# Attention's products of four pairs in one visit, 55 tanh differences by accumulating DMAs, exponentials summed on ScalarE

## The chip, the cores and the metric

One NeuronCore of a Trainium2 chip runs the whole kernel. The metric is device time in microseconds (us), from the start of the execution to its end. TensorE multiplies matrices; VectorE (DVE), ScalarE (ACT) and GpSimd (POOL) work elementwise; SyncE (SP) issues most DMAs, and POOL issues the DMAs that add to their destination. Each engine works off its own list of instructions in the order in which the program wrote them.

## The reference

Attention over chunks of 64 tokens, then a feed-forward network whose activation is h - tanh(h):

```python
scores = scale * np.matmul(q_c, k_c.transpose(0, 1, 2, 4, 3))   # per head and chunk, 64 x 64
scores = scores - np.max(scores, axis=-1, keepdims=True)
attn = np.exp(scores)
attn = attn / (np.sum(attn, axis=-1, keepdims=True) + 1e-09)
x = np.matmul(attn, v_c)          # to 4608 tokens x 512 (8 heads of 64)
h = x @ w_in                      # 512 -> 2048
g = h - np.tanh(h)
out = g @ w_out                   # 2048 -> 512
```

## The kernel before

**Tiles.** The 4608 tokens are 36 pairs of chunks (128 tokens each), and four pairs form a group; there are nine groups. A number is kept as a sum of two 16-bit floats, so a product takes three matmuls. Groups 2 to 8 compute x @ w_in by Winograd's scheme: a unit (four per group, so units 8 to 35) has seven products (`gx` to `gw`, 12 matmuls of 128x256 each, line 798) that gather in three PSUM banks X, Y and Z. Four chunks n = 4 unit + 0..3 of 128x512 numbers are then made from the banks.

**A chunk's steps.** `sc` (ScalarE copies one bank), `st` (VectorE adds bank X), `sn` (ScalarE's tanh), `su` (the difference h - tanh, line 837 on VectorE), `sh` and `sl` (high and low half for the next product, ScalarE and VectorE). For a chunk in the list `ADDED` the difference is no VectorE instruction: a DMA issued by POOL adds the (negated) tanh to the chunk in SBUF (line 836), the copy and the sum apply the scale instead, and tanh runs without one. The second product is `K` (groups 2 to 4, 6 matmuls of 128x512, line 955) or, in groups 5 to 8, again seven Winograd products: sums of chunks `na`, their halves `nh` and `nl`, products `kp` (6 matmuls of 128x256, line 901) and joins `kj` (lines 914 and 917).

**Attention of a late pair p (8 to 35).** `S` computes the scores: 32 matmuls of 64x64 into both banks of the PSUM tile psa (line 208). `m` takes the row maxima on VectorE, `E` the exponentials on ScalarE, `z` divides by the row sums on VectorE, `h` and `l` split into halves, `t` transposes by DMA, `V` multiplies by the values: 48 matmuls of 64x64 (line 449), from pair 12 on into banks X and Y. Four drains `X p.0` and so on move the result from X and Y to SBUF on ScalarE (line 461). Bank Z is the first bank of psa, so a unit's first product into Z (`gz`) waits until the scores in psa have been read, and `gy` and `gx` wait for the drains.

**Two ways to the exponentials.** For a pair in `SUMMED`, ScalarE reads the scores from PSUM head by head: eight exponentials with the maximum as bias, each summing its row (line 402), which leaves VectorE the maxima (line 391) and a small scaling (line 393). For the others VectorE first subtracts the maxima from PSUM into SBUF (line 395), ScalarE takes one exponential of 128x512 in SBUF (line 404), and VectorE sums the rows (line 410).

**The order** is written out by hand as the string `SECOND`: each engine receives its instructions in the order of the tokens, whatever the other engines do. A visit is called here a stretch of 64x64 matmuls on TensorE between matmuls of 128x128. From pair 12 on before has 29 visits: three of them hold the values of two pairs and the scores of the next two (`V12 V13 S14 S15`, and the same for 14 to 17 and 16 to 19); of the other 26 one holds two pairs' values and one pair's scores, four hold two pairs' values, two hold two pairs' scores, eight hold the values of one pair and eleven the scores of one pair.

**Blocks of w_out.** `te` (blocks_out) stores differences of weight blocks to DRAM, `tr` and `tx` (blocks_back) read them back, two DMAs each.

Of the kernel before, what the change touches and what calls it, by code (L numbers as in the profile page):

```python
# [14 lines left out]
F16 = mybir.dt.float16  # L15
# [6 lines left out]
P = 128  # L22
# [8 lines left out]
FC = DFF // P  # L31
# [10 lines left out]
UNITS = 4  # L42
# [16 lines left out]
ORDER = (0, 1, 3, 6, 9, 5, 7, 10, 8, 2, 4, 13, 15, 14, 12, 11)  # L59
BESIDE = 12  # L60
MORE, SUMS, BLOCKS, TURNED, CS = 0, 4, 8, 12, 14
SUMMED = (8, 9, 10, 11, 24, 25, 26, 27, 28, 29, 30, 31, 32, 33, 34, 35)
SEVEN = (5, 6, 7, 8)
ADDED = [n for n in range(64, 132) if n % 4 in (0, 1)]
RELOADED = range(24, 36)
# [24 lines left out]
def attn_ffn_kernel(ctx: ExitStack, tc: tile.TileContext, qkE, vE, qL, kL, vL, w_in, w_out, out):  # L90
# [8 lines left out]
    nc = tc.nc  # L99
# [11 lines left out]
    wt, half_w, w_pool = [[None, None] for _ in range(FC)], [[None] * FC for _ in range(2)], {}  # L111
# [13 lines left out]
    def freed(k, dtype=F16):  # L125

        return place_of("h", 1, ORDER[k], dtype)
# [3 lines left out]
    def new_x():  # L131
        return tuple(xpool.tile([P, KC, MOST], F32R, name=f"x{a}") for a in "hl")
# [170 lines left out]
    class Late:  # L303
# [81 lines left out]
        def less(self, p):  # L385
# [5 lines left out]
            nc.vector.reduce_max(out=mx.rearrange("p (hp u) one -> p hp (u one)", hp=4), in_=d["ps"], axis=AX.X)  # L391
            if p in SUMMED:
                nc.vector.tensor_scalar_mul(mx, mx, -scale)
# [3 lines left out]
        def exponents(self, p):  # L397
            d = self.st[p]
            s = d["s"]
            if p in SUMMED:  # L400
                for h in range(H):
# [4 lines left out]
        def shares(self, p):  # L406
            d = self.st[p]
            s, sm = d["s"], d["sm"]
            if p not in SUMMED:
                nc.vector.reduce_sum(out=sm[:, :, 0], in_=s, axis=AX.X)  # L410
# [72 lines left out]
    class Half:  # L483
# [93 lines left out]
        def blocks_out(self, j):  # L577
            t = self.t16[j].rearrange("p a (k n) -> p a k n", k=4)
            nc.sync.dma_start(out=half_w[0][2 * j + 1][:, :, :2 * P], in_=t[:, :, 0])
            nc.sync.dma_start(out=turned_out[:, j], in_=t[:, :, 1:])  # L580

        def blocks_back(self, u, k):

            for s in range(2):
                nc.sync.dma_start(out=self.block(u, s, k), in_=turned_out[:, 2 * (u % UNITS) + s, :, k - 1])
# [177 lines left out]
    class Winograd:  # L763
# [21 lines left out]
        def middle(self, unit):  # L785
            self.m5 = late.tile([P, MOST], F32, name="m5", bufs=1)
            if 4 * unit + 3 in ADDED:
                nc.scalar.activation(self.m5, self.banks["Z"], AF.Copy, scale=self.ff(4 * unit).sig)
# [24 lines left out]
        def copied(self, n):  # L813
            if n % 4 < 3:
                c, bank = self.place(n)[0], self.banks["YZY"[n % 4]]
                if n in ADDED:
                    nc.scalar.activation(c, bank, AF.Copy, scale=self.ff(n).sig)
# [3 lines left out]
        def summed(self, n):  # L821
            c = self.place(n)[0]
            other, op = self.m5 if n % 4 == 3 else c, ALU.subtract if n % 4 == 2 else ALU.add
            if n in ADDED:
                nc.vector.scalar_tensor_tensor(out=c, in0=self.banks["X"], scalar=self.ff(n).sig, in1=other, op0=ALU.mult, op1=op)
# [3 lines left out]
        def tanh(self, n):  # L829
            t = self.now[n][2] = ffn.tile([P, MOST], F32, name="t", bufs=3)  # L830
            nc.scalar.activation(t, self.now[n][0], AF.Tanh, scale=-1.0 if n in ADDED else self.ff(n).sig)

        def less(self, n):
            c, _, t, _ = self.now[n]
            if n in ADDED:
                return nc.gpsimd.dma_start(out=c, in_=t, accum_op=ALU.add)  # L836
# [166 lines left out]
    spots = Spots()  # L1003
    x, nx = new_x(), new_x()
# [63 lines left out]
    def add(h, l):  # L1068

        if len(adding) >= PACE:  # L1070
            nc.gpsimd.tensor_copy(tick, adding[-PACE])
        nc.gpsimd.dma_start(out=h, in_=l, accum_op=ALU.add)  # L1072
        adding.append(h[:1, :1] if len(h.shape) == 2 else h[:1, 0, :1])

    def whole_x():
        add(nx[0].bitcast(F32), nx[1].bitcast(F32))

    def late_parts():
        raw_pool.close()
        pool = ctx.enter_context(tc.tile_pool(name="att", bufs=1, side="right", reuse_waits="tile"))  # L1080
        early_psum.close()
        side = ctx.enter_context(tc.tile_pool(name="side", bufs=1, reuse_waits="tile"))
        dram = ctx.enter_context(tc.tile_pool(name="dram", bufs=1, space=bass.MemoryType.DRAM))
        return side, dram, pool, ctx.enter_context(tc.tile_pool(name="ps_a", bufs=1, space=PSUM, side="right", reuse_waits="tile"))

    with tc.manual_schedule(engines={E.SP, E.PE, E.DVE, E.Activation, E.Pool}):
        nc.scalar.activation(pool.tile([P, 1], F32, name="tiny", bufs=1), warm[:, :1], AF.Exp)
        wholes = {}
        for token in PLAN.split():
            if token[0] == "W":  # L1090
                if token == "Wx":
                    whole_x()
                else:
                    part, fc = map(int, token[1:].split("."))
                    h, l = (t.bitcast(F32) for t in wt[fc][part])
                    add(h, l)
                    wholes[part, fc] = h
            else:
                step(token)
        side, dram, late, ps_a = late_parts()  # L1100
        turned_out = dram.tile([P, FC // 2, 2, 3, 2 * P], F16, name="turned")
        parked = dram.tile([P, UNITS, 7, 2, 2, 2 * P], F16, name="parked")
        ps_o2 = pools[0]
        att, half = Late(late), Half(late)
        for (part, fc), h in wholes.items():
            half.w[part][fc] = h
        sums_w16 = [{} for _ in range(UNITS)]
        spare = late.tile([P, DM], F32, name="spare", bufs=1)
        before, x, sources = ff, nx, nx
        own.update({(0, 2): lambda: spare, (1, 0): lambda: freed(15, F32)})  # L1110
        x = tuple(nx[1].bitcast(F16).rearrange("p kc n -> p (kc n)").rearrange("p (a kc n) -> a p kc n", a=2, kc=KC)[a] for a in range(2))
        nx = new_sums_of_x()
        now = dict(x=nx)

        def second(g_):
            ff = now["ff"] = FeedForward(1, x)
            ff.room(ps_o1, range(2))
            ff.room(ps_o2, range(2, 4))
# [49 lines left out]
        def stage(name):  # L1168
            return lambda *n: getattr(now["w"], name)(*n)

        steps = dict(
            wA=half.tops, wB=half.powers, x=top, Q=third, ff=ready, xA=lambda: att.tops(1), xB=lambda: att.powers_of_tops(1), f=lambda: second(1), M=more,
            Cx=x_high, Dx=x_low, e=lambda t: before.scaled(t), o=lambda t: before.store(t),
            W=half.whole, C=lambda part, fc: half.convert(part, fc, (0,)), D=lambda part, fc: half.convert(part, fc, (1,)),
            G=lambda fc: now["ff"].gemm1(fc, 0, 4), P=lambda fc: now["ff"].gemm2((fc, 0)),
            i=lambda fc: now["ff"].tanh((fc, 0)), j=lambda fc: now["ff"].less((fc, 0)), k=lambda fc: now["ff"].high((fc, 0)), q=lambda fc: now["ff"].low((fc, 0)),
            a=att.load, v=att.load_values, u=att.largest, rA=att.tops, rB=att.powers_of_tops, s=att.split_high, d=att.split_low,
            S=att.scores, m=att.less, E=att.exponents, z=att.shares, h=att.shares_high, l=att.shares_low, t=att.turned, V=att.products,
            ee=lambda g, t: (now["ff"] if g == 1 else now["w"].ffs[g]).scaled(t), oo=lambda g, t: (now["ff"] if g == 1 else now["w"].ffs[g]).store(t), fb=power_of_third,
            gz=product("Z", 3, 3, True), gy=product("Y", 1, 1, True), gx=product("X", 0, 0, True), gu=product("Z", 6, 2), gv=product("X", 4, 4), gw=product("Y", 2, 6, True), gq=product("X", 5, 5),  # L1180
            mc=stage("middle"), K=stage("chunk"), sc=stage("copied"), st=stage("summed"), sn=stage("tanh"), su=stage("less"), sh=stage("high"), sl=stage("low"),
            ta=half.blocks_in, tb=half.blocks_sum, tc=half.blocks_split, te=half.blocks_out, tr=half.blocks_back, tx=lambda unit: half.blocks_back(unit, 1), wp=half.park, wl=stage("reload"), wn=half.norm_of_values, wr=half.norms_of_values, wt=half.largest_row, ww=half.norm_of_weights, wg=half.norm_of_g,
            na=stage("sum"), nh=stage("sum_high"), nl=stage("sum_low"), kp=stage("seventh"), kj=stage("join"), ks=stage("store"),
            X=result, T=half.sum, c=lambda u, k: half.slot(u, k, (0,)), b=lambda u, k: half.slot(u, k, (1,)))
        for token in SECOND.split():
            if token[0] == "0":
                step(token[1:])
                continue
            kind, numbers = re.fullmatch(r"([a-zA-Z]+)([\d.]*)", token).groups()
            steps[kind](*(int(n) for n in numbers.split(".") if n))  # L1190


# [43 lines left out]
```

## Time and profile before

| | before |
|---|---|
| time, median of 3 runs | 777.9 us (777.27 to 778.21) |
| the profiled execution's own time | 777.72 us |
| its span, first to last instruction | 775.7 us |
| TensorE matmuls busy | 763.6 us, 98% |
| VectorE busy | 693.5 us, 89% |
| ScalarE busy | 549.3 us, 71% |
| GpSimd busy | 77.4 us, 10% |

The profiled execution took 2.0 us more than its span, the part outside the first and last instruction. Matmuls overlap one another: a 128x256 one is shown 273 ns long and a 128x512 one 379 ns, and the next starts before it ends, so TensorE's busy share says little, and times on TensorE are better taken from start to start. Instructions of VectorE and ScalarE overlap a little too.

### The profile page before, as it was taken

Reading aid. Unit: us, or ns where it says so; the run is one execution under the profiler, and the core shown is the slowest. Engines: PE = TensorE matmul, PEld = TensorE weight load, DVE = VectorE, ACT = ScalarE, POOL = GpSimd, SP = SyncE. Lnnn points to the kernel's source line nnn. Section 1 sums busy time; section 2 is a strip of 40 time slices with the busy share of each in tenths; the row PEclk is TensorE's granted clock in tenths of the full one; section 3 lists DMA queues with packets and bytes.
Section 4 is the critical chain, followed back from the end, with each engine's and each line's share of the span. In section 5 each row is a group of like instructions: output and inputs, shape, how many; then the busy total and the mean of one; then the engine's idle time right before and its main releaser. Section 6 shows DMA issues by size and latency. Waiting matters only on the chain.

```text
span 775.7 us, 19620 instructions
## 1 busy us (share of the span) xinstructions
PE 763.6 (98%) x7895; PEld 568.6 (73%) x7898; DVE 693.5 (89%) x1302; ACT 549.3 (71%) x1229; POOL 77.4 (10%) x117
## 2 busy tenths in 40 slices
PE   8999999999999999999999999999999999999998
PEld 3777885444476666667676767878888888888887
DVE  7999999999999998999999989999978896889761
ACT  6989887877566665666566869786968586777631
POOL 0022235300000000000110020101010001010000
PEclk9999999999999999999999999999999999999999
DMA  9977978733142403414857887578499459565111
GB/s 352 363 211 202 255 185 168 146 91 97 41 97 52 127 2 93 139 56 124 242 160 210 247 194 173 137 179 213 131 252 176 130 136 246 137 165 171 60 42 55
DMA packets 102123, 121.35 MB, mean 156 GB/s; under 512 B 36368, under 2 KB 59280, under 8 KB 101904
## 3 DMA queue, kind: packets, MB, share of 16 engines
q1 hardware_dynamic: 92240, 101.67, 43.9%
q0 software_dynamic: 9648, 18.35, 14.2%
q8 instruction: 62, 1.02, 0.5%
q14 instruction: 29, 0.24, 0.1%
q10 hardware_dynamic: 144, 0.07, 0.0%
HBM read 73.40 MB, written 19.92 MB: 120 GB/s over the span
## 4 chain that ended last, share of the span: by engine, by line
PE 84%; issue 8%; DMA 3%; DVE 3%; POOL 1%; ACT 1%; SPq 1%; POOLq 0%
PE ph L798 20%; PE po L955 16%; PE po L901 14%; PE po L726 11%; PE ph L681 11%; PE psa L798 8%; PE psa L208 2%; DMA gl<-t 1%; DMA v<-vE 1%; PE ph L449 1%; PE ps L208 1%; PE ph L1052 1%; DMA rawv<-vL 0%; POOL wh L836 0%; PE ps L199 0%
## 5 line engine op out<-in xcount | busy, mean ns | idle before, releaser
L798 PEld LDWEIGHTS <-wh 128*128 128x128 f16 x1344 | 130.9, 98 | 22.6 <-issue 2.0
L798 PEld LDWEIGHTS <-wl 128*128 128x128 f16 x1008 | 98.0, 98 | 17.8 <-issue 1.0
L798 PE MATMUL ph<-xh,wl 128*128 128x256 f16 x576 | 97.7, 273 | 0.0
L798 PE MATMUL ph<-xh,wh 128*128 128x256 f16 x544 | 92.7, 273 | 1.0 <-DVE gl L827 0.5
L798 PE MATMUL ph<-xl,wl 128*128 128x256 f16 x288 | 78.5, 273 | 0.0
L798 PE MATMUL ph<-xl,wh 128*128 128x256 f16 x272 | 74.2, 273 | 0.0
L901 PE MATMUL po<-wl,wh 128*128 128x256 f16 x564 | 72.1, 273 | 1.1 <-ACT wh L860 0.5
L901 PEld LDWEIGHTS <-wh 128*128 128x128 f16 x660 | 63.7, 98 | 9.6 <-ACT wh L860 0.8
L955 PE MATMUL po<-wl,gl 128*128 128x512 f16 x288 | 68.3, 379 | 0.0
L955 PE MATMUL po<-wl,gh 128*128 128x512 f16 x288 | 68.3, 379 | 0.0
L726 PE MATMUL po<-wl,gh 128*128 128x512 f16 (+1 forms) x192 | 63.3, 384 | 0.0
L798 PE MATMUL psa<-xh,wh 128*128 128x256 f16 x352 | 60.0, 273 | 0.2 <-ACT s L402 0.2
L955 PEld LDWEIGHTS <-gl 128*128 128x128 f16 x288 | 27.6, 98 | 29.0 <-DVE gl L851 0.2
L798 PE MATMUL psa<-xl,wh 128*128 128x256 f16 x176 | 48.0, 273 | 0.0
L955 PEld LDWEIGHTS <-gh 128*128 128x128 f16 x288 | 27.7, 98 | 27.4
L681 PE MATMUL ph<-xl,wl 128*128 128x512 f16 x192 | 43.1, 380 | 0.0
L402 ACT ACTIVATE s<-psa,mx 128x64 f32<-128x64 f32 x128 | 38.1, 338 | 2.2 <-DVE from L148 1.5
L466 DVE TENSOR_TENSOR xl<-wh,xh 128x512 f16<-128x512 f32 (+1 forms) x56 | 34.2, 617 | 2.0 <-ACT xh L466 1.8
L466 ACT CAST xh<-wh 128x512 f16<-128x512 f32 (+1 forms) x56 | 31.3, 575 | 5.5 <-DVE wh L474 3.9
L914 ACT ACTIVATE wh<-po,undo_g 128x256 f32<-128x256 f32 x32 | 15.0, 472 | 27.7 <-PE po L901 27.6
L681 PEld LDWEIGHTS <-wl 128*128 128x128 f16 x192 | 18.3, 97 | 21.9
L1072 POOL DMA_DIRECT2D wh<-wl x32 | 27.3, 853 | 63.6 <-DVE w L182 42.7
(322 smaller groups left out, 1885.1 us busy)
## 6 DMA issues: line engine op xcount, KB each, us to landing
wh<-parked SPq DMA_DIRECT2D x48, 256.0 KB, 3.1
wl<-parked SPq DMA_DIRECT2D x36, 256.0 KB, 3.5
raw<-w_in SPq DMA_DIRECT2D x16, 512.0 KB, 5.8
raw<-w_out SPq DMA_DIRECT2D x16, 512.0 KB, 6.6
wh<-wl POOLq DMA_DIRECT2D x32, 256.0 KB, 4.0
rawq<-qL SPq DMA_DIRECT2D x28, 256.0 KB, 3.6
rawk<-kL SPq DMA_DIRECT2D x28, 256.0 KB, 4.3
rawv<-vL SPq DMA_DIRECT2D x28, 256.0 KB, 3.5
```

The costliest lines, as they stand in the source:

```text
L208: nc.tensor.matmul(ps[os, r ^ o if crossed else r, hp * CH:(hp + 1) * CH], lhsT=lhsT(rs, hp, o), rhs=rhs(rs, hp, o), start=True, stop=True)
L402: nc.scalar.activation(s[:, h, :], d["ps"][:, h // 2, h % 2, :], AF.Exp, bias=d["mx"][:, h, :], scale=scale, accum_out=d["sm"][:, h, :])
L449: nc.tensor.matmul(ps[c][os, hp, :], lhsT=v[a][rs, c, hp, :], rhs=d["a16"][rs, b, hp, cs], start=(k == 0), stop=(k == 2), skip_group_check ...
L466: return (lambda: nc.scalar.copy(out=h, in_=a)), (lambda: nc.vector.tensor_sub(l, a, h))
L681: nc.tensor.matmul(ph, lhsT=self.weight(fc, 0, a)[:, kc * P:(kc + 1) * P], rhs=x[b][:, kc, cols], start=(k == 0), stop=(k == 3 * KC - 1))
L726: nc.tensor.matmul(self.po[t], lhsT=gg[a][:, ts], rhs=self.weight(fc, 1, b), start=(k == 0), stop=(k == 3 * FC - 1))
L798: nc.tensor.matmul(bank[:, q * 2 * P:(q + 1) * 2 * P], lhsT=self.weight(unit, a, i, q, kc), rhs=x[j][:, b, kc, :], start=(first and q == 0 ...
L901: nc.tensor.matmul(bank, lhsT=g[:, a, ts], rhs=w, start=id(t) not in begun, stop=(u == UNITS - 1 and s == 1 and a == 1), skip_group_check= ...
L914: nc.scalar.activation(to, self.half_of(g, 1, c), AF.Copy, scale=undo)
L955: nc.tensor.matmul(bank, lhsT=g[a][:, ts], rhs=half_w[1][fc][:, b, columns], start=(first and s == 0 and k == 0), stop=(last and s == 1 an ...
L1052: nc.tensor.matmul(idle, lhsT=warm[:, :P], rhs=warm, start=True, stop=True)
L1072: nc.gpsimd.dma_start(out=h, in_=l, accum_op=ALU.add)
```

## The change

Nothing is added to or taken from the tokens of `SECOND`: the same 2563 tokens stand in another order from the 310th on (some 195 us into the run). What differs:

- From pair 12 on, the values of two pairs and the scores of the next two always stand together: `V12 V13 S14 S15`, `V14 V15 S16 S17`, and so on to `V32 V33 S34 S35`, then `V34 V35`. That is 12 visits. The work around them is ordered anew.
- `SUMMED` holds all late pairs; the twelve pairs 12 to 23 are new in it.
- `ADDED` goes from 34 chunks to 55: in groups 2 to 4 chunks 0 and 2 of a unit (from chunk 34 on), in groups 5 and 6 chunks 0, 1 and 2, in group 7 chunks 0 and 1, in group 8 none (before: chunks 0 and 1 of a unit in groups 4 to 7 and of one unit of group 8).
- The block differences that `tx` reads back lie in a DRAM tensor of their own, so that one DMA of 256 KB reads what two of 128 KB read; `te` issues three DMAs where it issued two.

Of the two orders the diff shows the first place that differs and, as an example, the surroundings of `V26` with the whole stretch up to the next `gz` in the new order.

```diff
-0G11 ... k14 j12 m13 P15 k12 X9.8 q12 E13 ...
+0G11 ... k14 j12 m13 E12 E13 P15 k12 X9.8 q12 ...
...
-... V26 su90 sh88 kp21.3.1 su91 X26.3 sh90 kp21.3.0 sl88 X26.0 V27 sh91 ...
+... V26 V27 S28 S29 sl88 nh21.4 su91 X26.3 X27.9 X27.0 nl21.4 s30 a30 kp22.1.0 m28 sh91 a31 kp21.3.1 X26.0 d30 s31 gy23 sl91 wn30 m29 sh90 kp21.2.0 X26.1 na22.1 gx23 E29 wr30 wl24.2 X26.2 v34 kp22.1.1 na22.3 wl24.5 kp21.3.0 tx21 sl90 nh22.1 na22.2 nh22.3 kp22.2.0 kp22.2.1 nl22.1 E28 nl22.3 kp22.5.1 tx22 kp22.5.0 na22.4 u34 tx23 gz23 ...
-SUMMED = (8, 9, 10, 11, 24, 25, 26, 27, 28, 29, 30, 31, 32, 33, 34, 35)
+SUMMED = (8, 9, 10, 11, 12, 13, 14, 15, 16, 17, 18, 19, 20, 21, 22, 23, 24, 25, 26, 27, 28, 29, 30, 31, 32, 33, 34, 35)
-ADDED = [n for n in range(64, 132) if n % 4 in (0, 1)]
+ADDED = [n for n in range(34, 128) if n % 4 in {2: (0, 2), 3: (0, 2), 4: (0, 2), 5: (0, 1, 2), 6: (0, 1, 2), 7: (0, 1)}.get(n // 16, ())]
         def blocks_out(self, j):
-            nc.sync.dma_start(out=turned_out[:, j], in_=t[:, :, 1:])
+            nc.sync.dma_start(out=turned_thirds[:, j], in_=t[:, :, 1])
+            nc.sync.dma_start(out=turned_out[:, j], in_=t[:, :, 2:])
         def blocks_back(self, u, k):
             for s in range(2):
-                nc.sync.dma_start(out=self.block(u, s, k), in_=turned_out[:, 2 * (u % UNITS) + s, :, k - 1])
+                nc.sync.dma_start(out=self.block(u, s, k), in_=turned_out[:, 2 * u + s, :, k - 2])
+        def third_back(self, unit):
+            u = unit % UNITS
+            nc.sync.dma_start(out=spots.third(unit), in_=turned_thirds[:, 2 * u:2 * u + 2])
-        turned_out = dram.tile([P, FC // 2, 2, 3, 2 * P], F16, name="turned")
+        turned_out = dram.tile([P, FC // 2, 2, 2, 2 * P], F16, name="turned")
+        turned_thirds = dram.tile([P, FC // 2, 2, 2 * P], F16, name="turned3")
-            tx=lambda unit: half.blocks_back(unit, 1)
+            tx=half.third_back
```

## Rows read from the trace of the kernel before

**Rows 1.** Stages: us; busy PE, PEld, DVE, ACT, POOL; granted clock; DMA share, GB/s

```profile
225.00:342.00 117.00, 117.00 (x1244) 79.73 (x1243) 109.65 (x204) 71.86 (x125) 0.81 (x1) 1.00 0.28 79
342.00:464.00 122.00, 122.00 (x1317) 81.78 (x1319) 114.81 (x244) 83.39 (x177) 12.87 (x16) 1.00 0.69 184
464.00:664.00 200.00, 197.26 (x2499) 169.09 (x2489) 179.91 (x339) 155.32 (x385) 18.45 (x24) 1.00 0.72 179
```

**Rows 2.** Chain of work that ended last: start us, length us, engine, line

```profile
229.06 2.62 PE ph L798 x24
236.92 3.88 PE po L955 x18
```

**Rows 3.** TensorE in order of time: start us, us, line, operation, shapes, count

```profile
303.03 1.03 PE L955 MATMUL po<-wl,gh 128*128 128x512 f16 x4
...
305.96 0.61 PE L955 MATMUL po<-wl,gl 128*128 128x512 f16 x2
...
340.93 1.67 PE L955 MATMUL po<-wl,gl 128*128 128x512 f16 x7
...
343.44 0.39 PE L955 MATMUL po<-wl,gl 128*128 128x512 f16 x1
...
377.63 1.03 PE L955 MATMUL po<-wl,gh 128*128 128x512 f16 x4
...
379.22 0.39 PE L955 MATMUL po<-wl,gl 128*128 128x512 f16 x1
...
498.76 0.82 PE L901 MATMUL po<-wl,wh 128*128 128x256 f16 x6
...
500.02 0.39 PE L901 MATMUL po<-wl,stage 128*128 128x256 f16 x2
```

**Rows 4.** Waits of TensorE from 225 us on: total us, times, longest us

```profile
PE psa L798 <- ACT gh L817: 0.5, 1, 0.5
PE po L901 <- ACT wh L860: 0.5, 1, 0.5
PE po L901 <- DVE wh L862: 0.5, 1, 0.5
PE ph L798 <- DVE gl L827: 0.5, 1, 0.5
PE ph L798 <- DVE wh L825: 0.3, 1, 0.3
PE psa L798 <- ACT s L402: 0.2, 1, 0.2
```

**Rows 5.** Groups by line: xcount | busy us, mean ns | idle before, releaser

```profile
L404 ACT ACTIVATE s<-s 128x512 f32<-128x512 f32 x12 | 7.6, 630 | 3.8 <-DVE s L395 3.7
...
L837 DVE SCALAR_TENSOR_TENSOR spare<-spare,sig,t 128x512 f32<-128x512 f32 x22 | 16.4, 744 | 1.8 <-ACT t L831 1.8
...
L395 DVE TENSOR_TENSOR s<-psa,mx 128x512 f32<-128x512 f32 x12 | 8.3, 691 | 0.4
L410 DVE TENSOR_REDUCE sm<-s 128x8 f32<-128x512 f32 x12 | 8.1, 677 | 0.0
```

**Rows 6.** ScalarE in order of time (columns as in rows 3), pairs 28 and 29

```profile
502.52 0.65 ACT L461 ACTIVATE wh<-ph 128x256 f32<-128x256 f32 x2
503.05 0.73 ACT L365 ACTIVATE wh<-rawv,to 128x512 f16<-128x512 f32 x1
503.66 0.32 ACT L402 ACTIVATE s<-psa,mx 128x64 f32<-128x64 f32 x1
...
505.97 0.78 ACT L618 ACTIVATE rawv<-rawv,to 128x512 f32<-128x512 f32 x1
```

**Rows 7.** Line 836: who waited for its DMAs (us, times), and time to landing

```profile
  ACT gh L845: 3.1, 4
...
  ACT t L831: 0.3, 1
...
DMA to landing us min/median/max: 3.3/4.8/7.9
```

More of the change, by code (lines that the diff above doesn't have):

```diff
@@ L1181, in attn_ffn_kernel @@
             mc=stage("middle"), K=stage("chunk"), sc=stage("copied"), st=stage("summed"), sn=stage("tanh"), su=stage("less"), sh=stage("high"), sl=stage("low"),
-            ta=half.blocks_in, tb=half.blocks_sum, tc=half.blocks_split, te=half.blocks_out, tr=half.blocks_back, tx=lambda unit: half.blocks_back(unit, 1), wp=half.park, wl=stage("reload"), wn=half.norm_of_values, wr=half.norms_of_values, wt=half.largest_row, ww=half.norm_of_weights, wg=half.norm_of_g,
+            ta=half.blocks_in, tb=half.blocks_sum, tc=half.blocks_split, te=half.blocks_out, tr=half.blocks_back, tx=half.third_back, wp=half.park, wl=stage("reload"), wn=half.norm_of_values, wr=half.norms_of_values, wt=half.largest_row, ww=half.norm_of_weights, wg=half.norm_of_g,
             na=stage("sum"), nh=stage("sum_high"), nl=stage("sum_low"), kp=stage("seventh"), kj=stage("join"), ks=stage("store"),
```

2 lines of the change are left out of this document (1 added, 1 removed).

## The prediction

> **What bounds the kernel now.** I read the page's first part (in the table above), then busy time by stage, then the chain of work that ended last, then TensorE in order of time, and last TensorE's waits. From 225 to 464 us TensorE has work the whole time and the granted clock is 1.00, the upper level, 2.4 GHz; from 464 to 664 us it is idle for some 3 us [rows 1]. The chain there is one TensorE instruction after another: 18 matmuls of 512 columns in 3.88 us, 0.216 us each, and 24 of 256 columns in 2.62 us, 0.109 us each [rows 2]. No product is added or dropped, so the time can move by two things: what TensorE loses around its 64x64 visits, and what it loses in waits. VectorE stands close behind, busy 94% of both stages up to 464 us and 90% of the next; ScalarE is at 61%, 68% and 78% [rows 1].
>
> **The visits.** A visit's cost is the time from where the next matmul could have started (last start before it plus its step) to the first 128x128 start after it [rows 3]. Scores of one pair: 377.63 + 4 x 0.216 = 378.49, next start 379.22, so 0.73 us. Values of two pairs: 340.93 + 7 x 0.216 = 342.44 to 343.44, 1.00 us. Values of one pair: 498.76 + 6 x 0.109 = 499.41 to 500.02, 0.61 us. Four pairs at once: 303.03 + 4 x 0.216 = 303.89 to 305.96, 2.07 us; the other two of that kind, read in the same way, take 2.01 and 2.05, so 2.05. Two pairs' scores take 1.2 and the visit of three pieces 1.6. Apart, four pieces cost 2 x 0.73 + 2 x 0.61 = 2.7 us, together 2.05: each entry and exit that goes saves some 0.2 us.
> Before, the 29 visits cost 3 x 2.05 + 1.6 + 4 x 1.0 + 2 x 1.2 + 8 x 0.61 + 11 x 0.73 = 27.1 us. After, 11 full ones and one of two pairs' values cost 11 x 2.05 + 1.0 = 23.5 us. That is 3.6 us off TensorE, which nothing else can hide, since TensorE is the path; by the spread of the full visits (2.01 to 2.07) it is 3.3 to 4.0. I take 3.5.
>
> **The waits now.** Six waits on ScalarE and VectorE, all between 508 and 618 us, 2.5 us idle [rows 4]. From start to start each is 0.16 us longer, since a 256-column matmul is shown 273 ns long and steps by 109: 2.5 + 6 x 0.16 = 3.5 us, and gaps too short for that view bring it to about 4. Three of the six (0.5, 0.5, 0.2) fall within 3 us, behind the exponentials of pairs 28 and 29: ScalarE was late with the operands of `kp` and then with the scores that bank Z waited for. The VectorE ones (0.5, 0.5, 0.3; the first of them is the second of those three) come where VectorE is fullest.
>
> **Exponentials on ScalarE, twelve pairs.** On VectorE the subtraction and the row sum go, 8.3 + 8.1 us [rows 5], and twelve scalings of 8 columns come, so about 14 us less, all before 425 us. On ScalarE twelve 128x512 exponentials go (7.6 us [rows 5]) and twelve times eight short ones come: 503.66 to 505.97, 2.31 us a pair [rows 6], 27.7 us; 20 us more. From 225 to 464 us ScalarE goes from 155 of 239 us to 175, 73%: it hides there on the sum. What it does not hide is the place: psa was released by VectorE's subtraction, and is now released by ScalarE's last exponential, and `gz` waits for that.
>
> **Bank Z after each visit.** For the eleven visits with scores I add the TensorE work written between the visit and the next `gz`, and ScalarE's work up to the later of the two `E`. The hardest is the one after `V26 V27`: nine `kp` of 6 x 0.109 and two products of 12 x 0.109 cover 8.5 us. On ScalarE stand nine operations of 0.61 (503.05 to 503.66 [rows 6]; one is a cast, a little shorter), four drains of 0.53/2 (502.52 to 503.05 [rows 6]) and two pairs' exponentials: 5.5 + 1.1 + 4.6 = 11.1 us. ScalarE can begin once the values are done, some 1.1 us before TensorE's first matmul (two pairs' scores plus the exit), so it is 1.5 us short. Summed in this way, the visits from `V12` to `V32` are short by -0.6, -0.6, -0.8, 0.3, -0.1, -0.1, -0.3, 1.5, 0.2, -3.5 and -2.2 us. The positive ones add to 2.0 us. The same sum for pairs 28 and 29 in the old order gives about 1 us, and the trace shows 0.5 + 0.5 + 0.2 us idle [rows 4], 1.7 from start to start; so the method errs by under a microsecond, to the low side.
>
> **Differences by DMA.** 21 more chunks leave VectorE, 0.744 us each [rows 5], 15.6 us. With the exponentials VectorE falls from 224 of 239 us by 14 + 11 (15 of these chunks lie in groups 2 and 3) to 83% there. POOL gets 21 issues more, on an engine that is busy 0.8, 12.9 and 18.5 us in the three stages [rows 1]. The price is latency: a DMA lands 3.3 to 7.9 us after its issue, in the median 4.8 [rows 7], and `sh` stands in ScalarE's order with everything behind it. The order leaves mostly 5.2 us of TensorE work between tanh and `sh`, in both kernels. With 34 such DMAs ScalarE waited 10.6 us for them (six rows, first and last shown [rows 7]); 55 make it 17 us, 6.5 more. Bounds for TensorE: nothing, if ScalarE's free time takes it, and 6.5 us if every wait is passed on. Of TensorE's six waits only one is laid to ScalarE outside the exponentials (0.5 us [rows 4]), although ScalarE waited 10.6 us for DMAs, so I take nothing and keep 6.5 for a rival.
> The Trainium skill's page "DMA: Bandwidth & Descriptors" (section "Anatomy of one DMA, SWDGE (gpsimd) path") fits such a DMA by about 2.0 us plus its bytes over 436 GB/s, an estimate of 2.6 us for 256 KB. By that page these DMAs would always land before `sh` and the rival below would have no chance; the trace's 4.8 us, up to 7.9, decides against it.
>
> **The small edits.** Sixteen `tx` now issue one DMA where they issued two, eight `te` three where two: eight issues fewer on SP, whose queue TensorE never waited for from 225 us on [rows 4]: nothing. At the very end one join (c = 0) stands two `kp` before the last matmul where it stood three before; its store of 256 KB runs beside the last join and its stores: nothing, at most 0.3 us.
>
> **The sum.** Of the waits after, I expect 2.0 us behind the exponentials and about 2 us of the other kind (some 2 now; VectorE has more room, but between the visits `V26` and `V28` the order gives it about as much work as TensorE, as before): 4, as now. So the profiled execution's 777.7 becomes 777.7 - 3.5 = 774.2 us. The median of the runs shown is 0.2 us higher, which is within their spread.
>
> **The rivals.**
> *The waits go too.* VectorE has some 30 us less to do, and TensorE loses nothing behind it. For it: no wait at all from 225 to 464 us even at 94% [rows 1, 4]. Against it: three of the six waits are ScalarE's, and ScalarE gets more. Then 774.2 less the 4 us of waits: 770.2 us.
> *The waits eat the gain.* ScalarE arrives at each visit 0.5 us late: the sums above then fall short by 4.5 us in all instead of 2.0, and 1 us comes from VectorE where it is full: 774.2 + 3.5 = 777.7 us, no change. The change would do what it says on TensorE, and it would not show.
> *Slower: late differences hold bank Z.* A DMA lands late, `sh` holds ScalarE, the exponentials behind it are late, and `gz` finds the scores still unread. With ScalarE 1 us late at every visit the sums fall short by 8.4 us, 6.4 over the forecast: 780.6 us. From a lateness of about 0.85 us on the kernel is slower. For it: 55 DMAs, half of which land within 0.4 us of their due time or after it; against it: only some visits have such an `sh` ahead of the exponentials.
> *It does not do what it says:* a merged visit must wait for four pairs' operands and free banks at once. The three merged visits of before start without any wait; I give it no share of its own.
>
> **Chances.** Forecast (772.4 to 776.3) 0.40; waits gone 0.24; gain eaten 0.19; slower 0.17. A change of 0.2%, 1.6 us, is about what a measurement of this kernel can tell from none. Faster 0.64, the same 0.19, slower 0.17. The range runs from the first rival with the larger saving of the visits, 769.6, to short of the third, 779.8.
>
> **What would show it.** After: 12 stretches of 64x64 matmuls from 225 us on, of 2.0 to 2.1 us; VectorE's busy time 25 to 30 us lower, ScalarE's about 20 higher; TensorE's waits on line 402 about 2 us, the largest after `V26 V27`. I am wrong if full visits take over 2.2 us, or if waits on line 402 or on DMAs of line 836 add to more than 4 us or are absent.

## The result and the profile after

The changed kernel takes 782.8 us in the median of four runs (781.89 to 783.17), the kernel before 777.8 us in four runs beside them: a ratio of 1.0063, 95% interval 1.0046 to 1.0081. It is slower by 5 us; I had forecast 774.2 us and a range that ended at 779.8. The profiled execution of after took 783.17 us, its span is 781.4 us. Line numbers behind the first changed methods are 5 higher than before: the products `g*` are L803, `kp` L906, `K` L960, `sl` L856 and L867, the differences by DMA L841.

The busy times of the page, and the same three stages as [rows 1], columns as there:

```profile
PE 765.2 (98%) x7898; PEld 570.9 (73%) x7898; DVE 669.6 (86%) x1269; ACT 568.3 (73%) x1409; POOL 98.3 (13%) x138
...
225.00:342.00 117.00, 117.00 (x1241) 79.64 (x1240) 102.33 (x207) 84.53 (x219) 12.22 (x15) 1.00 0.45 104
342.00:464.00 122.00, 120.08 (x1252) 80.75 (x1251) 102.70 (x213) 83.19 (x216) 12.27 (x15) 1.00 0.67 181
464.00:664.00 200.00, 195.95 (x2440) 168.83 (x2438) 174.90 (x335) 157.15 (x399) 27.41 (x33) 1.00 0.78 191
```

VectorE has 23.9 us less to do, a little under the 25 to 30 worked out, and ScalarE 19.0 more. TensorE, which had no gap from 225 to 464 us, now has one of 2 us there. Its waits over the whole span (us in total, times, longest), the ones of the first 190 us left out; [rows 4] is the same view of before from 225 us on:

```profile
PE psa L208 <- issue: 2.6, 2, 1.5
PE po L731 <- DVE gl L719: 2.4, 1, 2.4
...
PE po L906 <- DVE wh L867: 1.2, 3, 0.4
PE psa L803 <- ACT s L402: 0.7, 1, 0.7
...
PE po L906 <- issue: 0.6, 1, 0.6
...
PE po L906 <- DVE wh L922: 0.4, 1, 0.4
PE ph L803 <- DVE wh L832: 0.2, 1, 0.2
...
PE ph L803 <- DVE spare L832: 0.2, 1, 0.2
```

Two of these are new in kind. The wait on L719 stands at 206 us, ahead of the first visit that I had added up. And "issue" is a gap in which TensorE waited for nothing that the profile names; it lies in the middle of a visit. TensorE in order of time, columns as in [rows 3]:

```profile
350.94 0.97 PE L449 MATMUL ph<-wh,wh 64*64 64x64 f16 x96
351.79 0.93 PE L208 MATMUL psa<-rawk,rawq 64*64 64x64 f32 x48
354.21 0.46 PE L208 MATMUL psa<-rawk,rawq 64*64 64x64 f32 x16 [1.49 <-issue]
...
505.13 0.98 PE L449 MATMUL ph<-wh,wh 64*64 64x64 f16 x96
505.99 0.81 PE L208 MATMUL psa<-rawk,rawq 64*64 64x64 f32 x38
507.94 0.67 PE L208 MATMUL psa<-rawk,rawq 64*64 64x64 f32 x26 [1.15 <-issue]
...
549.28 0.93 PE L906 MATMUL po<-wl,wh 128*128 128x256 f16 x7 [0.65 <-issue]
```

64 score matmuls are two pairs, 32 each: the gaps come after 48 and after 38 of them, in the middle of the second pair, where the order brings no new operand and no new bank. A third gap of 0.65 us stands behind the visit at 546 us, among the products (the row at 549.28). The other nine full visits take 1.99 to 2.14 us, start to start; these two take 3.76 and 3.50. So the twelve visits cost 26.8 us where I had 23.5; the 29 of before, taken start to start in the same way, cost 26.9.

The second place is 195 to 225 us: from the start of pair 13's scores to the first visit the same 194 matmuls take 31.3 us from start to start; before they took 27.0, so 4.3 us are lost here. The first and last rows of this stretch, before and then after:

```profile
198.69 0.70 PE L208 MATMUL psa<-rawk,rawq 64*64 64x64 f32 x32
...
225.67 0.26 PE L449 MATMUL ph<-wh,v16h 64*64 64x64 f16 x8
```

```profile
198.48 0.69 PE L208 MATMUL psa<-rawk,rawq 64*64 64x64 f32 x32
...
229.76 0.26 PE L449 MATMUL ph<-wh,v16h 64*64 64x64 f16 x8
```

ScalarE, VectorE and TensorE there, in order of time:

```profile
201.68 0.31 ACT L402 ACTIVATE s<-psa,mx 128x64 f32<-128x64 f32 x1 [1.74 <-DVE mx L391]
...
206.03 0.41 ACT L402 ACTIVATE s<-psa,mx 128x64 f32<-128x64 f32 x1
...
206.32 0.81 ACT L710 ACTIVATE gh<-t,to_g 128x512 f16<-128x512 f32 x1
...
207.17 1.41 DVE L719 SCALAR_TENSOR_TENSOR gl<-t,to_g,gh 128x512 f16<-128x512 f32 x2 [4.73 <-ACT gh L710]
...
205.60 0.59 PE L731 MATMUL po<-wl,gh 128*128 128x512 f16 x2
208.64 0.39 PE L731 MATMUL po<-wl,gl 128*128 128x512 f16 x1 [2.44 <-DVE gl L719]
```

The order has `E12 E13` ahead of `k12`, where before had them behind it. As both pairs are now summed on ScalarE, sixteen short exponentials of 0.29 us hold it from 201.68 to 206.32, 4.6 us. `k12` (L710) waits behind them, `q12` on VectorE waits 4.73 us for `k12`, `q14` stands behind `q12` in VectorE's order, and `P14` on TensorE needs `q14`. Behind the wait the clock falls. Three windows of after and, below, the middle one of the kernel with only this order put back (run order12); granted clock third from the end:

```profile
195.00:210.00 15.00, 12.56 (x93) 6.20 (x92) 10.13 (x22) 8.93 (x41) 0.38 (x1) 0.99 0.20 62
210.00:213.00 3.00, 3.00 (x8) 1.06 (x7) 2.93 (x8) 2.61 (x5) 0.00 (x0) 0.50 0.00 0
213.00:225.00 12.00, 11.91 (x87) 8.45 (x86) 10.31 (x21) 8.94 (x15) 0.00 (x0) 0.99 0.63 178
```

```profile
210.00:213.00 3.00, 3.00 (x16) 1.34 (x14) 2.68 (x8) 2.95 (x7) 0.00 (x0) 1.00 0.00 0
```

0.50 is the lower of the two levels, 1.2 GHz: 8 matmuls in 3 us, which at 0.216 us [rows 2] would have taken 1.7. So in this execution the wait costs 2.4 us and the clock behind it 1.3. The clock does not fall each time: of the four executions of after two show a mean granted clock of 0.997 and 0.998 over the span, and two 1.000, with 781.89 and 783.12 us.

### The profile page after: what moved, and what is told of

It is laid out like the page before. It is cut to its first block, busy times and chain, and to the rows that moved or that the text cites. A ratio compares the mean times of both kernels' runs of the same rounds, so it can differ in the third digit from the quotient of the medians.

```text
span 781.4 us, 19832 instructions
## 1 busy us (share of the span) xinstructions
PE 765.2 (98%) x7898; PEld 570.9 (73%) x7898; DVE 669.6 (86%) x1269; ACT 568.3 (73%) x1409; POOL 98.3 (13%) x138
## 4 chain that ended last, share of the span: by engine, by line
PE 80%; DVE 11%; DMA 3%; issue 3%; ACT 2%; POOL 0%; SPq 0%; ACTq 0%; POOLq 0%; DVEq 0%
PE ph L803 18%; PE po L906 15%; PE po L960 14%; PE ph L686 10%; PE po L731 10%; PE psa L803 7%; PE psa L208 2%; PE ph L449 1%; ACT s L402 1%; DMA raw<-w_out 1%; DMA wh<-t 1%; DVE xl L466 1%; DMA gh<-t 1%; DVE wh L867 1%; PE ps L208 1%
## 5 line engine op out<-in xcount | busy, mean ns | idle before, releaser
L803 PEld LDWEIGHTS <-wh 128*128 128x128 f16 x1344 | 131.4, 98 | 22.4 <-issue 2.4
L803 PEld LDWEIGHTS <-wl 128*128 128x128 f16 x1008 | 98.5, 98 | 16.6 <-issue 0.8
L803 PE MATMUL ph<-xh,wl 128*128 128x256 f16 x576 | 97.8, 273 | 0.2 <-DVE spare L832 0.2
L803 PE MATMUL ph<-xh,wh 128*128 128x256 f16 x544 | 92.6, 272 | 0.4 <-DVE wh L832 0.2
L803 PE MATMUL ph<-xl,wl 128*128 128x256 f16 x288 | 78.5, 273 | 0.0
L803 PE MATMUL ph<-xl,wh 128*128 128x256 f16 x272 | 74.1, 273 | 0.0
L906 PE MATMUL po<-wl,wh 128*128 128x256 f16 x564 | 71.3, 273 | 1.8 <-DVE wh L867 1.2
L906 PEld LDWEIGHTS <-wh 128*128 128x128 f16 x660 | 64.0, 98 | 10.9 <-DVE wh L867 3.0
L402 ACT ACTIVATE s<-psa,mx 128x64 f32<-128x64 f32 x224 | 67.2, 350 | 3.5 <-DVE mx L391 3.5
L960 PE MATMUL po<-wl,gh 128*128 128x512 f16 x288 | 68.6, 379 | 0.0
L960 PE MATMUL po<-wl,gl 128*128 128x512 f16 x288 | 67.9, 379 | 0.0
L803 PE MATMUL psa<-xh,wh 128*128 128x256 f16 x352 | 60.0, 273 | 0.7 <-ACT s L402 0.7
L402 ACT ACTIVATION_READ_ACCUMULATOR s<-psa,mx 128x1 f32 x224 | 54.2, 243 | 0.0
L960 PEld LDWEIGHTS <-gl 128*128 128x128 f16 x288 | 28.0, 98 | 29.2 <-DVE gl L856 0.3
L960 PEld LDWEIGHTS <-gh 128*128 128x128 f16 x288 | 27.9, 98 | 28.6 <-DVE gh L856 0.5
L803 PE MATMUL psa<-xl,wh 128*128 128x256 f16 x176 | 48.0, 273 | 0.0
```

The lines of the kernel that those rows point to most:

```text
L402: nc.scalar.activation(s[:, h, :], d["ps"][:, h // 2, h % 2, :], AF.Exp, bias=d["mx"][:, h, :], scale=scale, accum_out=d["sm"][:, h, :])
L803: nc.tensor.matmul(bank[:, q * 2 * P:(q + 1) * 2 * P], lhsT=self.weight(unit, a, i, q, kc), rhs=x[j][:, b, kc, :], start=(first and q == 0 ...
L906: nc.tensor.matmul(bank, lhsT=g[:, a, ts], rhs=w, start=id(t) not in begun, stop=(u == UNITS - 1 and s == 1 and a == 1), skip_group_check= ...
L960: nc.tensor.matmul(bank, lhsT=g[a][:, ts], rhs=half_w[1][fc][:, b, columns], start=(first and s == 0 and k == 0), stop=(last and s == 1 an ...
```

## The experiments

Theory A: the exponentials of pairs 12 and 13 ahead of `k12` cost the 4 us at 206 us. Theory C: in the visits TensorE runs out of instructions. For C speaks a count: the page has 62 packets of 16 KB on the queue "q8 instruction", and TensorE has 15,796 records of matmuls and loads, 255 to a packet. That these packets are TensorE's is inferred from this count. A full visit has 320 of them in 1.8 us, while the products need 14 us or more for 256. The rivals are late accumulating DMAs or a fuller ScalarE (B), and an operand or bank that the trace doesn't name (D). The DMA queues of after, first 351.6 to 351.8 us and then 273.3 to 273.5 us (packets, MB, share of 16 engines in this 0.2 us; only the place counts here):

```profile
q8 instruction: 1, 0.02, 40.2%
...
q8 instruction: 1, 0.02, 27.7%
```

The packet at 351.67 us starts 0.7 us into its visit, and TensorE resumes 2.5 us behind that start; the one at 505.32 starts 0.2 us into its visit, and TensorE resumes 2.6 us later. The one at 273.33 starts when its visit is over, and there is no pause. These three places suggest that a packet early in a visit makes the pause; pad128 below will show that its place in the visit is not what counts.

**Order alone (order12).**

```diff
-m13 E12 E13 P15 k12 X9.8 q12 q14 T1.3.1 G11 i11 j11 Q
+m13 P15 k12 X9.8 q12 E13 q14 T1.3.1 G11 i11 E12 j11 Q
```

> The changed kernel with the exponentials of pairs 12 and 13 put back behind k12 and q12, where the kernel before has them; nothing else differs. Theory A (ScalarE spends 4.6 us on the two pairs' exponentials before it gets to k12, so q12, q14 and then P14 are late, TensorE idles 2.4 us at 206 us and its granted clock falls to the lower level for some 1.5 us' worth of work): the wait and the lower clock go, 782.8 - 4.0 = 778.8 us (778.2 to 780.2). Rival B (the loss comes from accumulating DMAs that land late, or from the fuller ScalarE over the whole second half): at most 0.5 us, 782.3 to 782.8.

Measured: 779.0 us (ten runs, 776.89 to 780.01), ratio to before 1.0011 (1.0000 to 1.0021). The wait on L719 is gone and the granted clock is 1.00. 3.9 us go with two tokens; A stands and B falls. The stretch from pair 13's scores to the first visit takes 27.6 us here, 0.6 more than before, with a new wait of 0.42 us on VectorE (L832) at 220.7 us. Of what is left (TensorE, 225 to 664 us) the pauses are the largest rows, and the other waits add to no more than before's:

```profile
PE psa L208 <- issue: 2.2, 2, 1.6
PE po L906 <- issue: 0.8, 1, 0.8
PE psa L803 <- ACT s L402: 0.7, 1, 0.7
PE po L906 <- DVE wh L867: 0.6, 2, 0.4
```

**The two pairs unsummed (unsummed12).** `SUMMED` without 12 and 13, order as changed.

> The changed kernel with pairs 12 and 13 left out of the pairs whose exponentials sum on ScalarE; the order is the changed one. Theory A: their exponentials take 0.6 us each again, so k12 comes about 3.3 us sooner and P14 doesn't wait or waits under 0.3 us; VectorE has 2.4 us more around 205 us: about 779 us (778.3 to 780.5). If not the length of the exponentials but their place or P15's is what counts, TensorE still waits over 1.5 us at 206 us and the time stays above 781.5.

Measured: 780.0 us (778.17 to 781.34), ratio 1.0022 (1.0010 to 1.0034). About 3 us come back without the order being touched: it is the length of the exponentials ahead of `k12` that counts.

**Three visits cut (split3).**

```diff
-V18 V19 S20 S21 ... K56.0 ... K57.1
+V18 V19 K56.0 K57.1 S20 S21 ...
-V26 V27 S28 S29 ... s30 a30 kp22.1.0 m28 sh91 a31 kp21.3.1
+V26 V27 ... s30 a30 kp22.1.0 sh91 a31 kp21.3.1 S28 S29 m28
-V28 V29 S30 S31 ... kp20.7.1
+V28 V29 kp20.7.1 S30 S31 ...
```

> The changed kernel with the three visits that are followed by or hold a pause of TensorE (at 351, 505 and 546 us) split in two: two products of 1.3 us stand between the values and the scores in the first two, one in the third. Theory C (TensorE runs out of instructions: a visit of four pairs uses up 320 instructions in 1.8 us, and a 16 KB packet of the instruction queue begins within the visit at 0.2 to 1.2 us and TensorE goes on 2.3 to 2.6 us behind its start): the pauses of 1.5, 1.2 and 0.65 us go, three more entries and exits cost 0.25 us each: 782.8 - 3.3 + 0.7 = 780.2 us (779.4 to 781.0). Rival D (the scores wait for an operand or a bank that no semaphore row names): the pauses move with the scores or stay, 782.5 to 783.5.

In this kernel the scores of pairs 28 and 29 read the operands of 30 and 31, which are loaded ahead of them, and the join `kj5.1.2` reads a sum to which `kp20.7.1` is already added. Measured: 782.8 us, ratio 1.0070 (1.0047 to 1.0093), no gain; the time lies in rival D's range, though the pauses neither moved with the scores nor stayed, as D wanted. The two pauses inside the visits are gone (the halves take 1.00 and 1.19 us), and of the one behind the third 0.5 us is left. But the exponentials, and what waits for them, come no sooner. TensorE's largest waits, 190 to 664 us:

```profile
PE psa L803 <- ACT s L402: 2.5, 2, 1.7
PE po L731 <- DVE gl L719: 2.4, 1, 2.4
PE po L906 <- DVE wh L867: 1.7, 2, 1.3
```

So C was right about the pauses and wrong about the price: the scores still come late, the products moved in between are missing behind them, and the wait moves to bank Z. Behind this wait, at 360 us, the granted clock is 0.50 for some 3 us, while it stays 1.00 behind the wait at 206 us, which this kernel still has.

**Shifted against the packets (pad128).**

```diff
-            d["ps"] = quarters(...)
+            for _ in range(3 if p == 12 else 1):
+                d["ps"] = quarters(...)
```

> The changed kernel with the 64 TensorE instructions of pair 12's scores issued three times (the same result is written again): 128 more instructions at 198 us, and nothing else. Theory C: all later visits stand 128 instructions further on against the 256-instruction packets, so the pauses at 351, 505 and 548 us leave these visits and come up in the ones near 272, 436, 583 and 626 us, whose packets now start early in the visit. Time +0.9 us for the repeats and about one more pause, 784 to 786 us. Rival D: the pauses stay in the same three visits, since their operands are the same; 783.7 us.

Measured: 789.8 us in the one run. The pauses are gone from the visits that had them (now at 356, 511 and 550 us), and new ones stand elsewhere; a line of this kernel is one higher. The visit of pairs 14 and 15's values, which took 2.1 us in after, and the one at 356, which took 3.76:

```profile
271.18 0.98 PE L450 MATMUL ph<-wh,wh 64*64 64x64 f16 x96
272.03 1.04 PE L208 MATMUL psa<-rawk,rawq 64*64 64x64 f32 x54
276.33 0.39 PE L208 MATMUL psa<-rawk,rawq 64*64 64x64 f32 x10 [3.26 <-issue]
...
356.07 0.98 PE L450 MATMUL ph<-wh,wh 64*64 64x64 f16 x96
356.92 1.16 PE L208 MATMUL psa<-rawk,rawq 64*64 64x64 f32 x64
358.01 1.25 PE L961 MATMUL po<-wl,gh 128*128 128x512 f16 x5
```

A second new pause, 2.57 us, is at 589 us, one of 0.67 follows the visit at 397, and the third in the waits is the small rest (0.24 us) of L208's 6.1 us. Of the four visits that I had named two pause; of the other two (436 and 626) the first does not and the second hardly. The same operands, the same banks, only with 128 more instructions ahead of them in the stream: D falls, C stands. But the packets do not start early in these visits, as I had said: the one for the pause at 273 us starts at 273.88, 2.70 us into its visit and 0.8 us after TensorE stopped, and TensorE resumes 2.45 us behind it (the DMA queues of pad128, 273.8 to 274.0 us):

```profile
q8 instruction: 1, 0.02, 29.3%
```

What decides can be counted in the traces of all 13 kernels of this document, with TensorE's records (matmuls, weight loads, semaphore instructions) numbered in the order of their starts. All 26 pauses put down to "issue" after 190 us, in ten of the kernels, end at number 190 to 194 of a stretch of 256, which is one packet by the count above, and 2.2 to 2.7 us behind the start of a packet. Of the 118 full visits the 23 that begin 14 to 100 records ahead of such a number pause inside or within 3 us behind; none of the other 95 does. The other three pauses stand in visits that a run cut in two.

The time of pad128 rose by more than I said, in one run: 0.9 us for the repeats, 3.6 for longer pauses, and some 2.5 that other waits took.

**Order repaired and three visits moved (visits_moved).**

```diff
+... K56.0 K57.1 su59 sh58 sl58 sh59 K58.1 V18 V19 S20 S21 ...
+... V28 V29 S30 S31 kp23.5.1 wl25.5 st98 kp23.6.1 st99 ...
+16 instructions of pair 26's scores a second time
```

> The changed kernel with both repairs: the exponentials of pairs 12 and 13 behind k12 and q12 as in the kernel before, and the three visits moved against the packets of the instruction queue: the one at 351 us behind three products (36 instructions), the one at 546 us ahead of three products, and 16 instructions of pair 26's scores issued twice in the visit before the one at 505 us (0.1 us). Theory C (instruction supply): the pauses at 348 to 351, 504 and 545 us (1.56, 0.69 and 0.76 us beside the order repair alone) are gone; with the pause at 504 gone the product that waits 0.74 us for the exponentials at 514 waits about 1.4: 779.0 - 3.0 + 0.1 + 0.7 = 776.8 us (776.0 to 777.5). Rival D (the pauses stand for late operands or banks): they come back as waits with a name, 778.3 to 779.3.

Here the sums of chunks 98 and 99 read banks in which values and scores already lie. Measured: 783.3 us, ratio 1.0057 (1.0044 to 1.0071). No visit pauses inside any more, and the twelve cost 23.6 us, the 23.5 of the prediction; one pause of 0.9 us still follows the third. Yet by the ratios the kernel is 3.6 us slower than order12: with three products moved ahead of the visit at 351 us too little stands behind it, so that `K59.1` waits 1.9 us for its low half and bank Z 1.7 us for the exponentials (TensorE, 225 to 664 us).

```profile
PE psa L803 <- ACT s L402: 2.6, 2, 1.7
PE po L960 <- DVE gl L856: 1.9, 1, 1.9
```

**Values ahead of their visit (values_early).** Behind the order repair, `V18 V19`, `V26 V27` and `V28 V29` two or three products earlier, scores in place.

> The changed kernel with the order repair (exponentials of pairs 12 and 13 behind k12 and q12) and with the values of the three visits at 351, 505 and 546 us moved ahead of the two, three and three products before them, so that these products stand between values and scores; the scores, their exponentials and all work of the other engines keep their places. Theory C: a visit cut in two no longer outruns the instruction queue, the pauses of 1.6, 0.7 and 0.8 us go, each cut costs 0.15 us (1.00 and 1.19 us for the halves in an earlier run against 2.04), and the product that waits 0.74 us at 514 us waits up to 1.4: 779.0 - 3.0 + 0.45 + 0.3 = 776.7 us, 776.0 to 777.6; this would be faster than both kernels or the same as the kernel before. Rival D (operands or banks): the pauses come back under other names, over 778.3.

The sums of chunks 59, 91, 98 and 99 read banks that the values have already overwritten. Measured: 777.5 us (twelve runs, 776.04 to 780.93), ratio 0.9994 (0.9981 to 1.0007): by the ratios 1.3 us less than order12, about as much as the two intervals leave open (they overlap), inside Theory C's range, and no different from before. That the smaller pauses give time back when the scores stay in place is suggested, not shown. And it is no kernel to keep: the banks are not free that early. In order12 the sum of chunk 59 ends at 347.3 us and the visit starts at 347.7.

**Products between values and scores (values_between).** Behind the order repair, `K56.0`, then `kp22.1.0 kp22.1.1`, then `kp20.7.1 kp20.7.0` between the values and the scores of the three visits.

> The changed kernel with the order repair (exponentials of pairs 12 and 13 behind k12 and q12), and later products of 0.7 to 1.3 us put between the values and the scores of the three visits: one at 351 us, two at 505 us, two at 546 us; everything else keeps its place. Theory C (instruction supply): the pauses of 1.6, 0.7 and 0.8 us shrink to 0 to 0.3 us each, as TensorE now takes longer over the packet at hand; the three cuts cost 0.15 us each, and the scores come no later than they did behind the pauses, so the exponentials and the products behind them don't wait longer: 779.0 - 3.0 + 0.4 (rests of pauses) + 0.45 = 776.8 us, 776.0 to 777.8. Rival D (operands or banks): the pauses stay, before or behind the products moved in, and the time is 779 or more.

The joins of the sixth group read sums to which unit 20's products `kp20.7` are added too early. Measured: 781.5 us (780.03 to 783.56), ratio 1.0052 (1.0037 to 1.0066): a miss. The halves with scores take 1.75, 1.53 and 1.61 us instead of 1.19, so rests of 0.6, 0.3 and 0.4 us stay of the pauses, and the waits for the exponentials rise to 2.0 us and for the low halves (L867) to 1.2, as in split3. No run here beats the kernel before.

**The parts on the other engines.** Four runs ask what the prediction had at nothing. The accumulating differences of before, 34 in place of 55, behind the order repair (`ADDED` as before):

> The order repair alone, with the 34 accumulating differences of the kernel before in place of 55; VectorE gets 15.6 us back. Theory of the prediction (the further 21 differences neither cost nor give anything while TensorE is the bound): 779.0 us, 778.4 to 779.6. Rival (differences that land late hold the high halves and the products behind them): 1.0 to 1.5 us faster, 777.5 to 778.0, and the waits for the halves by lines 865 and 867 shrink. Second rival (VectorE needs the relief): its halves come later, over 780.

Measured: 791.7 us, ratio 1.0172 (1.0157 to 1.0186), over the second rival's bound. ScalarE's waits for DMAs (342 to 464 us) and, below, what TensorE waited for (225 to 664 us):

```profile
ACT gl L850 <- DMA t<-t: 5.6, 1, 5.6
...
ACT gl L850 <- DMA spare<-t: 4.6, 1, 4.6
```

```profile
PE po L960 <- ACT gh L850: 3.3, 1, 3.3
...
PE po L960 <- ACT gl L850: 1.4, 1, 1.4
```

Here chunks whose `sh` the order sets close behind the difference go by DMA, and of the 10.2 us that ScalarE waits for two late landings 4.7 reach TensorE by name. Then the set of after from chunk 64 on alone (`range(64, 128)`):

> The order repair alone, and of the 55 accumulating differences only the 40 from chunk 64 on; the 15 of the chunks 34 to 63 are VectorE's again (+11 us of it between 225 and 400 us). The run with the 34 of the kernel before lost 9 us at 415 to 437 us, where it has other chunks by DMA than the order was written for, and 1.1 us ahead of 400 us. Theory E (what that run lost is an order written for another set of differences: a difference that lands 4 to 5 us late where VectorE's was awaited): this kernel, whose set from chunk 64 on is the order's, loses only the 1.1 us: 780.1 us, 779.3 to 780.8. Rival (VectorE needs the relief as such): 785 or more, with waits of TensorE for halves all along. The prediction's own step (a cost of nothing): 779.0.

Measured: 781.1 us (779.39 to 783.79), ratio 1.0036 (1.0022 to 1.0051), 2 us over order12 and 0.3 over Theory E's range. The 9 us at 415 to 437 us are gone, so they came from the mismatch; and without the 15 early differences by DMA this order loses 2 us rather than nothing. As the order was written with them, the run does not separate VectorE's relief from another, smaller mismatch. Then the 16 summed pairs of before (`SUMMED` as before) behind the order repair:

> The order repair alone, with the 16 summed pairs of the kernel before: pairs 12 to 23 go back to four passes of VectorE (+14 us of VectorE, -20 us of ScalarE between 200 and 470 us). The prediction's step (the exponentials' move neither costs nor gives while TensorE is the bound): 779.0, 778.4 to 779.6. If the emptier VectorE is what lets the merged visits run without waits, 780 to 784 with waits for halves and exponentials; if the fuller ScalarE costs, 777.5 to 778.3.

Measured: 786.6 us, ratio 1.0102 (1.0082 to 1.0122), 7 us over order12 and over all that I expected, with VectorE behind in places where it was not (225 to 664 us):

```profile
PE ph L803 <- DVE wh L830: 2.0, 2, 1.4
PE psa L803 <- ACT m L795: 1.7, 2, 1.2
...
PE ph L803 <- DVE spare L830: 1.0, 2, 0.8
```

And the kernel before with eight more pairs summed, in its own order (`SUMMED` with 12 to 15 and 20 to 23):

> The kernel before, in its own order, with the exponentials of eight more pairs (12 to 15 and 20 to 23) summed on ScalarE: ScalarE +8 x 1.67 = 13.4 us, VectorE -8 x 1.17 = 9.4 us. Theory A and the prediction (the exponentials cost nothing where no short chain waits behind them; in this order those of pairs 12 and 13 stand behind k12 and q12): 777.7 us, 777.2 to 778.2. Rival B (the fuller ScalarE as such makes halves late): 778.5 to 780, with new waits of TensorE for the halves of lines 851 and 860.

Measured: 788.0 us, ratio 1.0117 (1.0092 to 1.0142), far over both expectations, and one row holds most of it (200 to 664 us; line 798 is the `g*` products of before):

```profile
PE psa L798 <- ACT s L402: 7.5, 4, 3.0
```

The exponentials now read bank Z itself, and an order written for a subtraction that clears it early lets the next product wait for up to 3 us.

## Why the prediction was wrong

Two steps failed. The 3.5 us that the visits were to save did not come, since pauses that the sum didn't know took as much; and the exponentials, put at nothing outside the visits, cost 3.9 us at a place ahead of the first one.

**The visits.** The count and the cost of a visit were right: nine of eleven full ones take 1.99 to 2.14 us against 2.01 to 2.07. The sentence "which nothing else can hide, since TensorE is the path" failed, and so did the rival that I gave no share: I asked only whether four pairs' operands and banks would be there. Some 320 instructions in 1.8 us outrun their own supply when the visit begins 14 to 100 records ahead of the end of a stretch of 256; before, the three full visits begin some 4, 132 and 225 ahead of it. That was luck, and I took these three for all. Without pauses the twelve cost 23.6 us (visits_moved), 3.3 less than before; two visits took 3.1 us more than their kind and a third pause 0.65, which gave it all back. That the whole kernel would be 3 us faster without pauses is not shown: split3 and visits_moved, which take them away, lose as much or more in other waits. My own mark for "wrong", full visits over 2.2 us, is met by 3.76 and 3.50.

**The exponentials.** ScalarE's 20 us were right (19.0). "What it does not hide is the place" was the right question, but I asked it of bank Z alone and from the visit of pair 12 on. What else stands behind `E` on ScalarE I didn't look up, and at 201 us that was `k12`, with `q12`, `q14` and `P14` behind it. This one place costs 3.9 us (order12).

**Bank Z.** The sums behind the visits gave 2.0 us of waits on line 402, the largest behind `V26 V27`; the trace has one of 0.7, there. That term was on the high side, and the pause in the visit before it doesn't explain why: the wait is 0.7 us as well in order12, where that pause is 0.69 us instead of 1.15, and 0.9 in visits_moved, where there is none. The cause stays open. (The slower rival's 8.4 us is 8.5 by the terms shown, which changes nothing.) That lateness there is dear was right, as split3, visits_moved and before_sum8 show.

**Differences by DMA.** A cost of nothing was right for the order as written: ScalarE waits 11.2 us for them (10.6 before, I had 17), and TensorE doesn't wait for one by name. The slower rival's mechanism exists, as order12_added34 shows, but not in this kernel. That it makes no difference which engine has this work was wrong for this order: 2 us for 15 of the differences in order12_added40, and 7 us for the twelve pairs in order12_summed16. I had taken an idle share for slack; in a fixed order a VectorE that is 14 us fuller is late at single places. What the relief is worth in an order written for the fuller VectorE was not measured.

**The waits without the pauses** add from 225 us on to 2.7 us in the view, line 402's 0.7 among them, and to about 4 from start to start, as forecast in sum.

**The sum.** From before's 777.7: the visits with their pauses -0.1, the pause behind one +0.65, 195 to 225 us +4.3, make 782.6; the profiled execution took 783.2. The rest of 0.6 us I did not trace to a cause; part of it lies in low halves (L867, 1.2 us after; 0.5 for the same line before [rows 4]). Order12's last 1 us over before holds the 0.6 us ahead of its first visit; the rest stays open. My four cases spanned 769.6 to 780.6 and had one idea in common: that what is slower must come from ScalarE at a visit.

## What to carry to other kernels

When a change makes an operation longer on an engine with room, list what stands behind it in that engine's order at each place where it occurs, the first ones too; the share of idle time says nothing of this. When small matmuls are packed closer, count instructions per microsecond and not only engine time, and number them, to see where in a stretch of 256 each dense part begins: three good examples prove little if their phase is luck. A repair that moves work across a chain must move the chain's start forward; otherwise the pause comes back as a wait under another name.

## What the runs showed of the hardware

By the count, TensorE's instructions come in packets of 16 KB, some 256 each, during the run. In or just behind dense visits TensorE stood still (0.2 to 3.3 us idle, 26 times) until 2.2 to 2.7 us behind the start of such a packet and went on at number 190 to 194 of a stretch of 256 records; moving the stream by 128 instructions moved the pauses to other visits.

After the idle time of 2.4 us at 206 us the granted clock was 0.50 for some 3 us in the profiled execution of after; behind the pauses of 1.5 and 1.2 us the windows of [rows 1]'s kind stay at 1.00. The same wait of 2.4 us in split3 and pad128 was not followed by a lower clock, nor was pad128's pause of 2.57 us, while that of 3.26 us was (0.50 from 276.8 to 280.2 us); what decides between them no run here shows. From pair 13's scores to the first visit these two took 29.6 and 30.3 us, against 31.3 with the lower clock. The Trainium skill's page "TensorE: Matmul & The Clock Gate" (section "Part 1: The HAM clock gate (the "warmup" mystery)") has the clock at 1.2 or 2.4 GHz by how busy the engine has been; the row of 0.50 agrees. With the order repaired there is neither this wait nor the lower clock.
